# Attention ahead of two MoE layers: one transpose bank for keys and queries, kept keys, later first conversions, low parts on VectorE

## The chip, the core and the metric

The kernel runs on one core of a Trainium2 chip. The metric is the device time of one execution in microseconds. The core has TensorE (PE, matmuls; PEld are its weight loads), VectorE (DVE), ScalarE (ACT), GpSimd (POOL) and SyncE (SP, which only issues DMAs here). Each engine runs its own instructions in the order in which they stand and waits on semaphores for the others. TensorE's results go to PSUM; in this kernel VectorE and ScalarE read them from there.

## The reference

```python
# q, k, v: (2, 8, 768, 64); 4 sink keys; a window of 128
scores = scale * q @ k.T                       # causal, window 128, or one of the first 4 keys
a = softmax(where(keep, scores, -1e9)); attn = a @ v
x = attn as (1536, 512)
h = x @ w_in                                   # (512, 2048)
x = where(h >= 1, h, where(h <= -1, 0, (h + 1)**2 / 4)) @ w_out
h = x @ moe2_w_in
out = where(h > 0, h, exp(min(h, 0)) - 1) @ moe2_w_out
```

All in fp32. The four weight matrices arrive in a wider format, as pairs of 32-bit words, and are converted to fp32 on the chip.

## The kernel before

**Matmuls.** A product of the MoE is made of three passes: an operand is split into a high part (`xh`, `wh`, `gh`, a rounding to fp32r on ScalarE) and a low part (`xl`, `wl`, `gl`, the rest, a subtraction), and high x high, high x low and low x high are added up in PSUM.

**Attention (`Attn`).** Queries go in *segments* of two blocks of 128 rows: six in all, three for each of the two batches, and in each segment four *pairs* of heads. The 24 (segment, pair) *jobs* run in the order of `self.jobs`; pairs and jobs are counted from 0 here, so "pair 4" is the first pair of the second segment. A job has five stages, staggered over the jobs by a table in `stages`:

- T (`st_T`): TensorE transposes the natural blocks of keys (three blocks, the one ahead of the segment included; two in a batch's first segment) into a bank `kps` and of queries (two) into `qps`. Each bank is copied to SBUF (`kT`, `qT`; L471), by VectorE ahead of the MoE, by ScalarE later. GpSimd keeps the sink keys (`sk`, L478) and puts them behind each key block (L479).
- S0, S1 (`st_S`): scores of a query block (L504). VectorE masks them and finds the row maximum (L508), ScalarE exponentiates (L510), GpSimd copies the sinks' weights (L513).
- X (`st_X`): the weights are transposed and copied by ScalarE (L539).
- V (`st_V`): product with the values, copied to `xb` by VectorE (L565). `xb` has one buffer for all segments.

When a segment's four pairs are through, `st_sink` adds the sinks and divides (L601, L602 on VectorE), and writes the MoE's input as `xh` (L604, ScalarE) and `xl` (L605, GpSimd).

**MoE (`Moe`).** 96 items, (layer, 512 tokens, 128 of the 2048 hidden columns); item i takes 12 matmuls into `h` (L171) and 12 of item i-2 into `y` (L210), with the activation between (L178 to L188 in the first layer; L180 on VectorE ends it). The first layer needs 32 *conversion units*, each a block of a weight matrix: two ScalarE activations (L138, L139) of the loaded words `st`, and on VectorE L142, L143 and L145, which writes `F`. The items' loop asks for them three items ahead. `wsplit` makes `wh` (L158, ScalarE) and `wl` (L160: VectorE in the first 16 items, GpSimd later).

**What sets the order.** The first two segments run ahead of the MoE (`attn.spare` holds its idle PSUM banks for them). The later ones are pulled in between the MoE's matmuls, `go(n=1)` at each of some four places of an item. Ahead of the MoE TensorE's order is as written; elsewhere a list scheduler orders each engine's instructions when the program is built. The only hold on it is `issue_after`: instructions built under `self.queue(e)` are ordered behind a given one. `self.behind` holds the last exponential and the last masking of the first segment's first job; before, it is applied to unit 1 alone:

```python
after = self.behind if self.n_cv == 1 else self.own if self.n_cv > 2 * self.KF else None
```

Of the kernel before, what the change touches and what calls it, by code (L numbers as in the profile page):

```python
# [7 lines left out]
F32 = mybir.dt.float32  # L8
# [4 lines left out]
ALU = mybir.AluOpType  # L13
# [5 lines left out]
NSINK = 4  # L19
BLK = 128  # L20
KW = BLK + NSINK
# [5 lines left out]
def f32(ap):  # L27
    return ap.bitcast(F32)
# [36 lines left out]
class Moe:  # L65
# [46 lines left out]
    def queue(self, e):  # L112


        after = self.behind if self.n_cv == 1 else self.own if self.n_cv > 2 * self.KF else None
        return self.tc.issue_after(after[e]) if after else nullcontext()

    def convert(self, n):
# [163 lines left out]
class Attn:  # L282


    def __init__(self, tc, ctx, q, k, v, xts, idn, const, segs, nq=2):
        self.tc, self.nc = tc, tc.nc
        nc = self.nc
        self.q, self.k, self.v, self.xts = q, k, v, xts
        self.B, self.H, self.S, self.D = q.shape
        self.scale = 1.0 / float(self.D) ** 0.5  # L290
        self.idn, self.const = idn, const
        self.nq = nq
        pool = lambda n, b, **kw: ctx.enter_context(tc.tile_pool(name="a_" + n, bufs=b, **kw))
        self.ld_p = pool("ld", 3)
        self.qk_p = pool("qk", 2)
        self.p_p = pool("p", 4)
        self.pt_p = pool("pt", 2)
        self.xb_p = pool("xb", 1)
        self.s_p = pool("s", 2)
        self.ps = pool("ps", 2, space=PSUM)  # L300
        self.sk = {}
        self.turn, self.spare = 0, []
        self.nat = {}
        self.first = None
        self.jobs = [(s, pr) for s in segs for pr in range(self.H // 2)]
        for what in "kq":
            self.load(what, *self.jobs[0])
# [81 lines left out]
    def load(self, what, seg, pr):  # L389
        nc, D, nq = self.nc, self.D, self.nq  # L390
        b, q0 = seg[0], seg[1]
        k0 = max(q0 - 1, 0)
        nk = q0 + nq - k0
        src, r0, n = {"q": (self.q, q0, nq), "k": (self.k, k0, nk), "v": (self.v, k0, nk)}[what]
        t = self.ld_p.tile([128, n, 2, D], F32, tag=what + "n", name=what + "n")
        for j in range(2):

            (nc.scalar if what == "q" and (seg, pr) in self.jobs[:2] else nc.sync).dma_start(  # L398
                out=t[:, :, j, :],
                in_=src[b, 2 * pr + j, r0 * BLK:(r0 + n) * BLK, :].rearrange("(n p) d -> p n d", p=128))  # L400
        self.nat[what, seg, pr] = t
# [54 lines left out]
    def st_T(self, seg, pr, st):  # L456
        nc, D, nq = self.nc, self.D, self.nq
        b, q0 = seg[0], seg[1]
        qn, kn = (self.nat.pop((what, seg, pr)) for what in "qk")
        k0 = max(q0 - 1, 0)  # L460
        nk = q0 + nq - k0
        first = q0 == 0

        def parts(t, n, nm, w):

            bank = self.bank([128, n, 128], nm + "ps")
            for j in range(n):
                nc.tensor.transpose(bank[:, j, :], t[:, j].rearrange("p h d -> p (h d)"), self.idn)  # L468
            o = self.qk_p.tile([128, n, w], F32, tag=nm + "T", name=nm + "T")

            (nc.vector.tensor_copy if self.spare else nc.scalar.copy)(o[:, :, 0:BLK], bank)  # L471
            return o

        kT = parts(kn, nk, "k", KW)
        qT = parts(qn, nq, "q", BLK)
        if first:
            self.sk[pr] = self.const.tile([128, 1, NSINK], F32, tag=f"sk{pr}", name=f"sk{pr}")
            nc.gpsimd.tensor_copy(self.sk[pr], kT[:, 0:1, 0:NSINK])  # L478
        nc.gpsimd.tensor_copy(kT[:, :, BLK:], self.sk[pr].to_broadcast([128, nk, NSINK]))  # L479
        st["qk", pr] = qT, kT  # L480

    def st_S(self, seg, pr, st, n):
        nc, D, nq = self.nc, self.D, self.nq
        b, q0 = seg[0], seg[1]
        k0 = max(q0 - 1, 0)
        qT, kT = st["qk", pr]
        if n == 0:
            P = []
            nb = self.s_p.tile([128, nq, 2], F32, tag="nb", name="nb")
            st["P", pr] = P, nb  # L490
            if "sm" not in st:
                st["sm"] = self.s_p.tile([128, nq, self.H], F32, tag="sm", name="sm")
                st["ps"] = self.s_p.tile([128, nq, self.H * (NSINK + 2)], F32, tag="psn", name="psn")
        P, nb = st["P", pr]
        sm = st["sm"]
        P.append(self.p_p.tile([128, 2, WP], F32, tag="P", name="P"))
        qb = q0 + n
        ty = min(qb, 2)
        W = KW if qb == 0 else WP
        j0 = max(qb - 1, 0) - k0  # L500
        S = [self.bank([128, W], "S") for _ in range(2)]
        for h in range(2):
            hs = slice(h * D, (h + 1) * D)
            nc.tensor.matmul(S[h], lhsT=qT[hs, n, :], rhs=kT[hs].rearrange("p j k -> p (j k)")[:, j0 * KW:j0 * KW + W],  # L504
                             start=True, stop=True)
        for h in range(2):
            o = P[n][:, h, 0:W]
            dv = nc.vector.tensor_tensor_reduce(out=o, in0=S[h], in1=self.mask[ty], op0=ALU.add, op1=ALU.min,  # L508
                                                scale=-self.scale, scalar=3.0e38, accum_out=nb[:, n, h:h + 1])
            ac = nc.scalar.activation(o, o, AF.Exp, bias=nb[:, n, h:h + 1], scale=-1.0,  # L510
                                      accum_out=sm[:, n, 2 * pr + h:2 * pr + h + 1])
        sinks = st["ps"][:, n, 2 * pr * NSINK:2 * (pr + 1) * NSINK]
        nc.gpsimd.tensor_copy(sinks.rearrange("p (h s) -> p h s", h=2), P[n][:, :, BLK:KW])  # L513
        if n == nq - 1 and self.first is None:
            self.first = (ac.ins, dv.ins)

    def chunks(self, q0):
# [49 lines left out]
    def st_sink(self, seg, st):  # L567
        nc, D, nq = self.nc, self.D, self.nq
        b, q0, t, c0 = seg
        H = self.H  # L570
        R = H * NSINK
        N = nq * 128

        ps, sm = st["ps"], st["sm"]
        nc.vector.tensor_scalar(out=sm, in0=sm, scalar1=1.0e-9, scalar2=None, op0=ALU.add)
        nc.vector.reciprocal(out=sm, in_=sm)
        nc.vector.tensor_copy(ps[:, :, R:R + H].bitcast(F32R), sm)
        nc.vector.tensor_tensor(out=ps[:, :, R + H:], in0=sm, in1=ps[:, :, R:R + H], op=ALU.subtract)
        bank = self.bank([R + 2 * H, N], "sps")
        for n in range(nq):  # L580
            nc.tensor.transpose(bank[:, n * 128:(n + 1) * 128], ps[:, n, :], self.idn)
        pst = self.xb_p.tile([3 * R + 2 * H, N], F32R, tag="pst", name="pst")
        nc.scalar.copy(pst[0:R], bank[0:R])
        nc.scalar.copy(pst[2 * R:3 * R], bank[0:R])
        nc.scalar.copy(pst[3 * R:], bank[R:])
        nc.vector.tensor_tensor(out=pst[R:2 * R], in0=bank[0:R], in1=f32(pst[0:R]), op=ALU.subtract)
        xh, xl = self.xts[t]
        vs = self.vsink(b)
        yield
        for p2 in range(0, self.H // 2, 2):  # L590
            bank, rep = [self.bank([128, 2, N], nm) for nm in ("xps", "rps")]
            for j in range(2):
                h = 2 * (p2 + j)
                nc.tensor.matmul(bank[:, j, :], lhsT=vs[:, h:h + 2, :].rearrange("p h d -> p (h d)"), rhs=pst,
                                 start=True, stop=True)
            for j in range(2):
                h = 2 * (p2 + j)
                nc.tensor.matmul(rep[:, j, :], lhsT=self.one[:, h:h + 2, :].rearrange("p h d -> p (h d)"), rhs=pst,
                                 start=True, stop=True)
            x = st["xb"][:, p2:p2 + 2, :]  # L600
            nc.vector.tensor_tensor(out=x, in0=bank, in1=x, op=ALU.add)  # L601
            nc.vector.tensor_tensor(out=x, in0=x, in1=rep, op=ALU.mult)  # L602
            hi = xh[:, p2:p2 + 2, c0:c0 + N]
            nc.scalar.copy(hi, x)  # L604
            nc.gpsimd.tensor_tensor(out=xl[:, p2:p2 + 2, c0:c0 + N], in0=x, in1=f32(hi), op=ALU.subtract)  # L605
            yield


# [218 lines left out]
```

## Time and profile before

| | |
|---|---|
| time, median of 3 runs | 673.9 us (673.19 to 674.31) |
| time of the profiled execution | 674.09 us |
| its span, first to last instruction | 672.4 us |
| mean granted TensorE clock | 0.992 |
| busy: PE, PEld | 649.0 us (97%), 502.6 us (75%) |
| busy: DVE, ACT, POOL | 381.1 us (57%), 453.4 us (67%), 262.5 us (39%) |
| first 40th of the span (16.8 us): PE, ACT | 5 and 1 tenths busy |
| MoE's first matmul | at 61.19 us |

Some 61 us of attention are followed by the MoE with the rest of the attention in between. A busy share over the whole span mixes these stages; times below are from the start of the span.

### The profile page before, as it was taken

What the parts mean: (1) busy time and instruction counts of PE and PEld (TensorE: products, weight loads), DVE (VectorE), ACT (ScalarE), POOL (GpSimd) and SP (SyncE); (2) the same over time, 40 slices, a digit from 0 to 9 for tenths busy, and PEclk for the clock granted to TensorE, in tenths of its full rate; (3) what the DMA queues carried; (4) which work ended last, traced back from release to release, by engine and by line L of the source; (5) the groups of instructions that cost most, each with busy time, mean ns of one, the idle gap of its engine ahead of it and who ended that gap; (6) DMA issues with size and microseconds to landing.
All of it is one profiled execution on the core that took longest, in us unless ns stands there. A gap on an engine that the chain in (4) does not pass through costs nothing.

```text
span 672.4 us, 9284 instructions
## 1 busy us (share of the span) xinstructions
PE 649.0 (97%) x3104; PEld 502.6 (75%) x3104; DVE 381.1 (57%) x753; ACT 453.4 (67%) x928; POOL 262.5 (39%) x276
## 2 busy tenths in 40 slices
PE   5977999999999999999999999999999999999996
PEld 2665677767777767888878888888888888888884
DVE  4888999998345334223988778777432222322221
ACT  1988998997667665556868778776655555555542
POOL 2222013002114335543546555554544444444431
PEclk8899999999999999999999999999999999999999
DMA  7576564864210000000433232321010000100001
GB/s 178 133 185 177 167 180 144 223 185 122 52 24 13 13 0 1 2 0 1 156 106 115 94 97 93 100 90 61 1 62 1 0 1 0 64 1 0 1 0 68
DMA packets 71017, 48.95 MB, mean 73 GB/s; under 512 B 48944, under 2 KB 65328, under 8 KB 70960
## 3 DMA queue, kind: packets, MB, share of 16 engines
q1 hardware_dynamic: 69584, 48.00, 24.8%
q8 instruction: 26, 0.43, 0.3%
q10 hardware_dynamic: 1376, 0.26, 0.2%
q14 instruction: 31, 0.25, 0.1%
HBM read 45.11 MB, written 3.15 MB: 72 GB/s over the span
## 4 chain that ended last, share of the span: by engine, by line
PE 82%; DVE 8%; issue 3%; ACT 3%; SPq 1%; DMA 1%; POOL 1%; POOLq 0%; DVEq 0%; ACTq 0%
PE h L171 36%; PE y L210 35%; PE S L504 3%; PE ops L562 3%; PE tps L537 2%; DVE ca L143 1%; DVE P L508 1%; DVE F L145 1%; DVE wl L160 1%; DVE ca L142 1%; SPq L398 1%; PE y L267 1%; PE kps L468 1%; DVE xb L602 1%; DVE g L180 0%
## 5 line engine op out<-in xcount | busy, mean ns | idle before, releaser
L160 POOL TENSOR_TENSOR wl<-F,wh 128x512 fp32r<-128x512 f32 x160 | 219.6, 1377 | 236.7 <-ACT wh L158 220.5
L158 ACT CAST wh<-F 128x512 fp32r<-128x512 f32 x192 | 117.6, 618 | 104.4 <-PE h L171 96.2
L171 PE MATMUL h<-xh,wh 128*128 128x512 f32 x384 | 155.4, 405 | 0.3 <-DVE g L180 0.3
L171 PE MATMUL h<-xl,wh 128*128 128x512 f32 x384 | 150.7, 393 | 0.9 <-POOL xl L605 0.9
L171 PE MATMUL h<-xh,wl 128*128 128x512 f32 x384 | 151.0, 393 | 0.0
L187 ACT CAST gh<-g 128x512 fp32r<-128x512 f32 x96 | 59.6, 621 | 63.2 <-DVE g L184 36.1
L184 DVE SCALAR_TENSOR_TENSOR g<-g,h 128x512 f32<-128x512 f32 x48 | 33.0, 688 | 115.0 <-ACT g L183 115.0
L188 DVE TENSOR_TENSOR gl<-g,gh 128x512 fp32r<-128x512 f32 x96 | 68.7, 715 | 48.9 <-ACT gh L187 48.5
L171 PEld LDWEIGHTS h<-xh,wh 128*128 128x128 f32 x384 | 72.1, 188 | 20.2 <-issue 5.2
L171 PEld LDWEIGHTS h<-xh,wl 128*128 128x128 f32 x384 | 72.1, 188 | 16.7
L171 PEld LDWEIGHTS h<-xl,wh 128*128 128x128 f32 x384 | 72.2, 188 | 16.1 <-POOL xl L605 1.5
L210 PE MATMUL y<-gh,wh 128*128 128x512 f32 x192 | 79.2, 413 | 0.0
L145 DVE CUSTOM_DVE_ANT_0 F<-ca,F 128x1024 uint16<-128x1024 uint16 x64 | 73.1, 1141 | 5.2 <-DVE ca L143 1.8
L210 PE MATMUL y<-gh,wl 128*128 128x512 f32 x192 | 75.7, 394 | 0.0
L210 PE MATMUL y<-gl,wh 128*128 128x512 f32 x192 | 75.3, 392 | 0.0
L210 PE MATMUL y<-wh,gh 128*128 128x512 f32 x184 | 72.9, 396 | 0.0
L210 PE MATMUL y<-wh,gl 128*128 128x512 f32 x184 | 72.4, 394 | 0.0
L210 PE MATMUL y<-wl,gh 128*128 128x512 f32 x184 | 71.7, 389 | 0.0
L180 DVE SCALAR_TENSOR_TENSOR g<-h,g 128x512 f32<-128x512 f32 x48 | 33.0, 687 | 44.7 <-ACT g L179 44.4
L510 ACT ACTIVATE P<-P,nb 128x260 f32<-128x260 f32 (+1 forms) x96 | 46.5, 487 | 10.9 <-DVE nb L508 10.5
L513 POOL COPY psn<-P 128x8 f32<-128x8 f32 x48 | 12.1, 253 | 106.7 <-ACT P L510 101.4
L139 ACT ACTIVATE F<-st 128x512 int32<-128x512 uint32 x64 | 42.6, 669 | 12.4 <-DMA qn<-in_q_dram 11.9
(104 smaller groups left out, 911.9 us busy)
## 6 DMA issues: line engine op xcount, KB each, us to landing
st<-in_moe_w_in_dram SPq DMA_DIRECT2D x32, 512.0 KB, 3.9
st<-in_moe_w_out_dram SPq DMA_DIRECT2D x32, 512.0 KB, 3.7
kn<-in_k_dram SPq DMA_DIRECT2D x32, 96.0 KB, 2.2
vn<-in_v_dram SPq DMA_DIRECT2D x32, 96.0 KB, 2.3
out_dram<-o SPq DMA_DIRECT2D x12, 256.0 KB, 2.4
qn<-in_q_dram SPq DMA_DIRECT2D x44, 64.0 KB, 2.8
kn<-in_k_dram SPq DMA_DIRECT2D x16, 64.0 KB, 3.6
vn<-in_v_dram SPq DMA_DIRECT2D x16, 64.0 KB, 2.8
```

What stands on the lines that cost most here:

```text
L139: nc.scalar.activation(r, w0.bitcast(U32), AF.Copy, scale=2.0 ** -29)
L145: nc.vector.tensor_tensor(out=r, in0=ai, in1=r, op=ALU.add)
L158: nc.scalar.copy(hi, src)
L160: (nc.vector if i < self.KF else nc.gpsimd).tensor_tensor(out=lo, in0=src, in1=f32(hi), op=ALU.subtract)
L171: nc.tensor.matmul(h, lhsT=w[:, k * 128:(k + 1) * 128], rhs=x[:, k, c0:c0 + n], start=(k == 0 and p == 0), stop=(k == self.KD - 1 and p == 2))
L180: nc.vector.scalar_tensor_tensor(out=g, in0=h, scalar=1.0, in1=g, op0=ALU.max, op1=ALU.min)
L184: nc.vector.scalar_tensor_tensor(out=g, in0=g, scalar=-1.0, in1=h, op0=ALU.add, op1=ALU.max)
L187: ac = nc.scalar.copy(gh, g)
L188: dv = nc.vector.tensor_tensor(out=gl, in0=g, in1=f32(gh), op=ALU.subtract)
L210: nc.tensor.matmul(self.y[c], lhsT=a, rhs=b, start=(first and p == 0), stop=(last and p == 2))
L504: nc.tensor.matmul(S[h], lhsT=qT[hs, n, :], rhs=kT[hs].rearrange("p j k -> p (j k)")[:, j0 * KW:j0 * KW + W], start=True, stop=True)
L510: ac = nc.scalar.activation(o, o, AF.Exp, bias=nb[:, n, h:h + 1], scale=-1.0, accum_out=sm[:, n, 2 * pr + h:2 * pr + h + 1])
```

## The change

The blocks of keys and queries of a job are transposed into one PSUM bank and copied by one instruction into one tile `T`: entry 0 for the key block ahead, then two key blocks and two query blocks. The key block ahead is no longer loaded and transposed: it is the last key block of the same pair in the segment before, which GpSimd now copies aside (`kept`) and back into entry 0. Units 1 to 4 of the conversions are ordered behind the last exponential and the last masking of the third job (`self.jobs[2]`) instead of unit 1 behind the first. And `xl` of the segments that run ahead of the MoE is made by VectorE.

```diff
@@ Moe.queue
-        after = self.behind if self.n_cv == 1 else self.own if self.n_cv > 2 * self.KF else None
+        after = self.behind if self.n_cv <= 4 else self.own if self.n_cv > 2 * self.KF else None
@@ Attn.load
-        src, r0, n = {"q": (self.q, q0, nq), "k": (self.k, k0, nk), "v": (self.v, k0, nk)}[what]
+        src, r0, n = {"q": (self.q, q0, nq), "k": (self.k, q0, nq), "v": (self.v, k0, nk)}[what]
@@ Attn.st_T
-        def parts(t, n, nm, w):
-
-            bank = self.bank([128, n, 128], nm + "ps")
-            for j in range(n):
-                nc.tensor.transpose(bank[:, j, :], t[:, j].rearrange("p h d -> p (h d)"), self.idn)
-            o = self.qk_p.tile([128, n, w], F32, tag=nm + "T", name=nm + "T")
-
-            (nc.vector.tensor_copy if self.spare else nc.scalar.copy)(o[:, :, 0:BLK], bank)
-            return o
-
-        kT = parts(kn, nk, "k", KW)
-        qT = parts(qn, nq, "q", BLK)
+        lead = 0 if first else 1
+
+        bank = self.bank([128, 2 * nq, 128], "qkps")
+        for i, t in enumerate((kn, qn)):
+            for j in range(nq):
+                nc.tensor.transpose(bank[:, i * nq + j, :], t[:, j].rearrange("p h d -> p (h d)"), self.idn)
+        T = self.qk_p.tile([128, 1 + 2 * nq, KW], F32, tag="qkT", name="qkT")
+
+        (nc.vector.tensor_copy if self.spare else nc.scalar.copy)(T[:, 1:, 0:BLK], bank)
+        if pr not in self.kept:
+            self.kept[pr] = self.const.tile([128, BLK], F32, tag=f"kept{pr}", name=f"kept{pr}")
+        if lead:
+            nc.gpsimd.tensor_copy(T[:, 0, 0:BLK], self.kept[pr])
+        if q0 + nq < self.S // BLK:
+            nc.gpsimd.tensor_copy(self.kept[pr], T[:, nq, 0:BLK])
+        kT, qT = T[:, 1 - lead:1 + nq], T[:, 1 + nq:, 0:BLK]
@@ Attn.st_S
-        if n == nq - 1 and self.first is None:
+        if n == nq - 1 and (seg, pr) == self.jobs[2]:
             self.first = (ac.ins, dv.ins)
@@ Attn.st_sink
+        self.early = bool(self.spare)
...
-            nc.gpsimd.tensor_tensor(out=xl[:, p2:p2 + 2, c0:c0 + N], in0=x, in1=f32(hi), op=ALU.subtract)
+            (nc.vector if self.early else nc.gpsimd).tensor_tensor(out=xl[:, p2:p2 + 2, c0:c0 + N], in0=x, in1=f32(hi), op=ALU.subtract)
```

Three places where the built order differs. Line numbers of the changed program are one to three higher from `st_T` on (L510 is L511 there, L565 is L566, L604 on VectorE is the old L602).

ScalarE at the start of the program, before, from the query loads that it issues to the third pair's exponentials (`P`):

```order
L398 DMA qn<-in_q_dram 128x2x64 x4
L139 ACTIVATE F<-st 128x512
L510 ACTIVATE P,sm<-P,nb 128x132 x2
L510 ACTIVATE P,sm<-P,nb 128x260 x2
L379 CAST vpart<-vraw_190 32x64
L380 CAST vpart<-vraw_190 32x64
L138 ACTIVATE ca<-st 128x512
L510 ACTIVATE P,sm<-P,nb 128x132 x2
L510 ACTIVATE P,sm<-P,nb 128x260 x2
L539 COPY pt<-tps 128x384 x2
L139 ACTIVATE F<-st 128x512
L510 ACTIVATE P,sm<-P,nb 128x132 x2
```

and in the change, from the second pair's exponentials on:

```order
L511 ACTIVATE P,sm<-P,nb 128x132 x2
L511 ACTIVATE P,sm<-P,nb 128x260 x2
L540 COPY pt<-tps 128x384 x2
L379 CAST vpart<-vraw_192 32x64
L380 CAST vpart<-vraw_192 32x64
L511 ACTIVATE P,sm<-P,nb 128x132 x2
L511 ACTIVATE P,sm<-P,nb 128x260 x2
L540 COPY pt<-tps 128x384 x2
L138 ACTIVATE ca<-st 128x512
L139 ACTIVATE F<-st 128x512
L511 ACTIVATE P,sm<-P,nb 128x132 x2
L511 ACTIVATE P,sm<-P,nb 128x260 x2
```

These rows begin with the second pair's exponentials; ahead of them stand only the query loads, the first pair's exponentials and two small casts. Before, a conversion stood ahead of every pair's exponentials, the first pair's too; now the first two conversion activations stand behind the third pair's, ahead of pair 3's (the last two rows).

VectorE where the first segment's output is finished (L601, L602) and the next jobs go on, before:

```order
L601 TENSOR_TENSOR xb<-xps,xb 128x512 x2
L602 TENSOR_TENSOR xb<-xb,rps 128x512 x2
L471 COPY kT<-kps 128x3x128
L471 COPY qT<-qps 128x256
L508 ISA P,nb<-S,mask_152 128x260
L508 ISA nb 128x1
L508 ISA P,nb<-S,mask_152 128x260
L508 ISA nb 128x1
L565 COPY xb<-ops 128x256
```

and now:

```order
L603 TENSOR_TENSOR xb<-xps,xb 128x512 x2
L604 TENSOR_TENSOR xb<-xb,rps 128x512 x2
L469 COPY qkT<-qkps 128x4x128
L607 TENSOR_TENSOR xl_74<-xb,xh_73 128x2x256 x2
L509 ISA P,nb<-S,mask_152 128x260
L509 ISA nb 128x1
L566 COPY xb<-ops 128x256
```

Two copies have become one, and the two subtractions for `xl`, which GpSimd ran beside these rows, stand in VectorE's row ahead of the next segment's first copy into `xb`.

VectorE between the second segment's output and the MoE's first gate (L180), before:

```order
L602 TENSOR_TENSOR xb<-xb,rps 128x512 x2
L143 SCALAR_TENSOR_TENSOR ca<-st,ca 128x512
L142 TENSOR_SCALAR ca<-ca 128x512
L145 ISA F<-ca,F 128x1024
L565 COPY xb<-ops 128x256
L143 SCALAR_TENSOR_TENSOR ca<-st,ca 128x512
L142 TENSOR_SCALAR ca<-ca 128x512
L145 ISA F<-ca,F 128x1024
L143 SCALAR_TENSOR_TENSOR ca<-st,ca 128x512
L160 TENSOR_TENSOR wl_1026<-F,wh_1025 128x512
L145 ISA F<-ca,F 128x1024
L180 SCALAR_TENSOR_TENSOR g<-h,g 128x512
```

and now:

```order
L143 SCALAR_TENSOR_TENSOR ca<-st,ca 128x512
L607 TENSOR_TENSOR xl_74<-xb,xh_73 128x2x256 x2
L145 ISA F<-ca,F 128x1024
L566 COPY xb<-ops 128x256
L143 SCALAR_TENSOR_TENSOR ca<-st,ca 128x512
L160 TENSOR_TENSOR wl_1006<-F,wh_1005 128x512
L145 ISA F<-ca,F 128x1024
L160 TENSOR_TENSOR wl_1002<-F,wh_1001 128x512
L509 ISA P,nb<-S,mask_152 128x260
```

Counted from the program's start, eight conversion units were finished (L145) ahead of the first L180 before, and six now.

## Rows read from the trace of the kernel before

**Rows 1.** Busy time by stretch: us, PE (x) PEld DVE ACT POOL, clock, DMA.

```profile
70.00:162.00 92.00, 91.68 (x477) 65.59 (x476) 87.37 (x194) 85.70 (x197) 14.98 (x31) 1.00 0.62 174
...
162.00:260.00 98.00, 97.20 (x523) 70.51 (x522) 42.53 (x112) 64.03 (x149) 28.37 (x38) 1.00 0.10 23
```

**Rows 2.** Timeline at the start: start us, us, engine, line [idle before <-releaser].

```profile
9.53 0.30 DVE L508 CUSTOM_DVE_ANT_0 P<-S,mask 128x132 f32<-128x132 f32 x1
...
12.53 0.93 SPq L398 DMA_DIRECT2D qn<-in_q_dram  x2
...
15.14 0.66 ACT L139 ACTIVATE F<-st 128x512 int32<-128x512 uint32 x1 [11.89 <-DMA qn<-in_q_dram]
...
16.98 0.94 SPq L398 DMA_DIRECT2D qn<-in_q_dram  x2
...
18.24 0.63 PE L468 MATMUL kps<-idn,kn 128*128 128x128 f32 x2
...
21.79 0.69 DVE L145 CUSTOM_DVE_ANT_0 F<-ca,F 128x1024 uint16<-128x1024 uint16 x1
...
23.51 0.49 PE L468 MATMUL kps<-idn,kn 128*128 128x128 f32 x3
...
25.18 0.40 ACT L510 ACTIVATE P<-P,nb 128x132 f32<-128x132 f32 x1 [0.29 <-DVE nb L508]
```

**Rows 3.** DMA issues, 0 to 30 us: count, KB each, median us to landing.

```profile
st<-in_moe_w_in_dram SPq DMA_DIRECT2D x2, 512.0 KB, 5.7
...
qn<-in_q_dram SPq DMA_DIRECT2D x14, 64.0 KB, 2.4
```

**Rows 4.** The chain that ended last, in order of time: start us, us.

```profile
12.53 2.62 DMA qn<-in_q_dram
...
129.60 0.33 PE kps L468 x3
```

**Rows 5.** Timeline around the low parts of segments 0 and 1.

```profile
42.26 2.50 POOL L605 TENSOR_TENSOR xl<-xb,xh 128x512 fp32r<-128x512 f32 x2 [1.63 <-ACT xh L604]
...
44.80 0.42 DVE L565 COPY xb<-ops 128x256 f32<-128x256 f32 x1 [1.61 <-POOL xl L605]
...
45.83 0.42 DVE L142 TENSOR_SCALAR ca<-ca 128x512 int32<-128x512 int32 x1
...
61.13 3.04 POOL L605 TENSOR_TENSOR xl<-xb,xh 128x512 fp32r<-128x512 f32 x2 [0.88 <-ACT xh L604]
...
61.52 1.50 DVE L142 TENSOR_SCALAR ca<-ca 128x512 int32<-128x512 int32 x1
...
62.80 0.51 PE L171 MATMUL h<-xl,wh 128*128 128x512 f32 x1 [0.89 <-POOL xl L605]
...
62.95 1.78 DVE L145 CUSTOM_DVE_ANT_0 F<-ca,F 128x1024 uint16<-128x1024 uint16 x1
```

**Rows 6.** Groups by line: operation, count, busy us, mean ns, idle before.

```profile
L143 DVE SCALAR_TENSOR_TENSOR ca<-st,ca 128x512 int32<-128x512 int32 x64 | 46.1, 721 | 1.3
...
L539 ACT COPY pt<-tps 128x512 f32<-128x512 f32 (+1 forms) x48 | 24.3, 546 | 3.6 <-PE tps L537 3.4
...
L160 DVE TENSOR_TENSOR wl<-F,wh 128x512 fp32r<-128x512 f32 x32 | 23.1, 723 | 5.4 <-ACT wh L158 4.1 <-PE tps L537 1.0
...
L471 ACT COPY kT<-kps 128x384 f32<-128x384 f32 (+1 forms) x13 | 5.7, 439 | 0.4 <-PE kps L468 0.4
...
L471 DVE COPY kT<-kps 128x384 f32<-128x384 f32 (+1 forms) x11 | 5.5, 504 | 0.9 <-PE kps L468 0.8
...
L471 ACT COPY qT<-qps 128x256 f32<-128x256 f32 x13 | 4.8, 373 | 0.0
...
L471 DVE COPY qT<-qps 128x256 f32<-128x256 f32 x11 | 4.6, 416 | 0.0
...
L278 DVE COPY o<-y 128x512 f32<-128x512 f32 x6 | 4.1, 690 | 8.9 <-PE y L210 5.0 <-PE y L267 3.9
...
L718 POOL TENSOR_SCALAR_AFFINE_SELECT idn<-idn 128x128 f32<-128x128 f32 x1 | 0.3, 292 | 0.0
```

More of the change, by code (lines that the diff above doesn't have):

```diff
@@ L300, in __init__ @@
         self.ps = pool("ps", 2, space=PSUM)
-        self.sk = {}
+        self.sk, self.kept = {}, {}
         self.turn, self.spare = 0, []
@@ L459, in st_T @@
         qn, kn = (self.nat.pop((what, seg, pr)) for what in "qk")
-        k0 = max(q0 - 1, 0)
-        nk = q0 + nq - k0
         first = q0 == 0
-        def parts(t, n, nm, w):
-            bank = self.bank([128, n, 128], nm + "ps")
-            for j in range(n):
-                nc.tensor.transpose(bank[:, j, :], t[:, j].rearrange("p h d -> p (h d)"), self.idn)
-            o = self.qk_p.tile([128, n, w], F32, tag=nm + "T", name=nm + "T")
-            (nc.vector.tensor_copy if self.spare else nc.scalar.copy)(o[:, :, 0:BLK], bank)
-            return o
-        kT = parts(kn, nk, "k", KW)
-        qT = parts(qn, nq, "q", BLK)
+        lead = 0 if first else 1
[12 more added lines that the diff above has]
+        kT, qT = T[:, 1 - lead:1 + nq], T[:, 1 + nq:, 0:BLK]
         if first:
@@ L478, in st_T @@
             nc.gpsimd.tensor_copy(self.sk[pr], kT[:, 0:1, 0:NSINK])
-        nc.gpsimd.tensor_copy(kT[:, :, BLK:], self.sk[pr].to_broadcast([128, nk, NSINK]))
+        nc.gpsimd.tensor_copy(kT[:, :, BLK:], self.sk[pr].to_broadcast([128, nq + lead, NSINK]))
         st["qk", pr] = qT, kT
```

## The prediction

> **What bounds the kernel now.** I read the stretches first. From 70 to 162 us TensorE is busy for 91.68 of 92 us, VectorE for 87.37 and ScalarE for 85.70; from 162 to 260 us TensorE is still busy for 97.20 of 98, while VectorE has fallen to 42.53 and ScalarE to 64.03 [rows 1]. So from 70 us on the end is set by TensorE, and in the first of the two stretches the other two engines keep up with 4.6 and 6.3 us to spare. An edit can save time in three ways only: the MoE starts earlier, TensorE gets less to do after it, or a wait of TensorE goes.
>
> Next, the order in time at the start. VectorE's first softmax step (L508) is at 9.53, so ScalarE could run the first exponentials at about 10. It runs L139, the first weight conversion, at 15.14 after 11.89 us of idling, and only then the exponentials [rows 2]. The trace puts that wait down to a load of queries, but L139 reads `st`: the first `w_in` block, like the others in this stretch, takes some 5.7 us to land, against 2.4 for a pair's queries [rows 3]. L139 ends at 15.80, so pair 0's exponentials stand some 5.5 us behind a weight nobody needs yet. TensorE transposes pair 3 at 18.24 and pair 4 at 23.51, and pair 3's exponentials start at 25.18 [rows 2].
>
> Last, the low parts. GpSimd works on segment 0's `xl` from 42.26 for 2.50 us, and VectorE's copy into `xb` at 44.80 has waited 1.61 us for it, as `xb` has one buffer. Segment 1's run from 61.13 for 3.04 us; TensorE's first MoE matmul that reads `xl` waits 0.89 us, and under them L142 takes 1.50 us and L145 1.78 us [rows 5], where they take 0.42 [rows 5] and 0.69 [rows 2] otherwise.
>
> **The change part by part.**
>
> *Conversions behind the third pair.* The exponentials of pairs 0 and 1 move into ScalarE's idle stretch. How much comes through is set by the loads. SyncE's order does not change here. Pair 3's second query load is in by 15.15 [rows 4], so its transposes can move from 18.24 to 15.15. Pair 4's queries are issued from 16.98 [rows 2] and take 2.4 [rows 3]: 19.4 at the earliest. If TensorE needs the same 5.27 us between the two transposes as now (23.51 minus 18.24), pair 4 follows at 20.4. So pair 3's exponentials, behind pair 4 on TensorE, start 3.1 to 4.1 us earlier. Not all of it is gained. Ahead of them ScalarE's order now has two conversion activations instead of four, 2 x 0.66 = 1.3 us put off; VectorE's has none of the first unit's L142, L143 and L145, 0.42 + 0.72 + 0.69 = 1.83 us [rows 2, 5, 6]. That work comes back before or soon after the MoE begins. Net: 1.8 to 2.8 us on ScalarE, 1.3 to 2.3 on VectorE. Bounds: 0 if all comes back, 5.5 if the whole wait comes through. I take **-2.0**.
>
> *Low parts on VectorE.* Four subtractions of 0.72 us (L160 on VectorE, same shape [rows 6]) go to VectorE, +2.9 us of its time; its wait of 1.61 and the two stretchings of 1.08 and 1.09 go, -3.8 [rows 5]. At 44.8 the `xb` buffer comes free sooner: two subtractions end 1.44 us after the high parts, where GpSimd needs 2.50; of the 1.06 I take 0.6, since ScalarE also has to follow. At 62.80 TensorE's wait of 0.89 [rows 5] goes and the second low part, which ends at 64.17, comes well over 1 us sooner; I take 1.0. Together **-1.6**; bounds -0.9 (that wait alone) and -2.5 (1.61 + 0.89).
>
> *One bank for keys and queries.* Sixteen transposes go (one for each pair of the four segments that are not first in their batch); 0.33 for three is 0.11 us each [rows 4]. Twelve of them lie behind the start of the MoE, on TensorE's path: **-1.3**. The four others are hidden by ScalarE and VectorE. A copy of 128x512 out of PSUM takes VectorE 0.69 (L278) for 0.50 + 0.42 now, 11 times 0.23 = 2.5 us before the MoE; ScalarE 0.55 (L539) for 0.44 + 0.37, 13 times 0.26 = 3.4 us, two thirds of it between 70 and 162 [rows 6]. I count these at nothing on the end: they pay for work that is put off. If that cover were gone they would be worth up to 2.
>
> *The kept keys.* 32 copies of 128x128 are new on GpSimd. No row has this copy. From below, `affine_select` of the same shape takes 0.29 [rows 6]; from above, half of the two 128x512 subtractions' 2.50 is 1.25 [rows 5]. A copy has one input and the shape of the first: 0.3. In the first segment one stands between pair 0's keys and its scores, 0.3 us that vanish in the wait for pair 3's loads. In later segments the copy in waits only for its buffer, a pair ahead of its use. What can cost is VectorE being held, as it was for L142 and L145 [rows 5]. About eleven of the copies fall between 70 and 162 us. VectorE then has 24 of 32 conversion units (44 us) and some 26 L160 (19 us) to do, two thirds of its time, so up to 11 x 0.3 x 0.67 = 2.2 us. And it has two units more to catch up: eight L145 stand ahead of its first L180 now, six then, 2 x 1.83 = 3.7 us. Against 4.6 us of slack that is 1.3 too much; the 2.5 us saved on copies ahead of the MoE covers it, not fully where waits fall badly. I take **+0.5**; bounds 0 and 3.7.
>
> The Trainium skill (SBUF — State Buffer, "Who interferes with whom") says that VectorE and GpSimd share one port pair as an exclusive lock, held for a whole instruction, and that two-input VectorE operations on SBUF contend with a GpSimd operation that reads SBUF. That speaks for the low parts' move and against the kept copies; the trace agrees for L142, 1.50 for 0.42 us. By the rule alone, with each of the eleven copies holding VectorE up in full, they would cost 3.3 us (an estimate) for the 2.2 above.
>
> Sum: -2.0 - 1.6 - 1.3 + 0.5 = **-4.4 us**. The profiled execution took 674.09 us, 0.2 above the median of 673.9; 674.1 - 4.4 = **669.7 us**.
>
> **The rivals.** About 0.2% of the time, 1.35 us, is what a measurement here tells from no change.
>
> *The work comes back (20%).* VectorE's slack between 70 and 162 consists of short waits for other engines, and the 3.7 us put off do not fit into it. Then TensorE, full now, waits for gates and conversions by that much: 669.7 + 3.7 - 0.5 = 672.9, and 671.5 to 673.5 around it. For it: VectorE is at 95% there [rows 1]. Against: conversions run three items ahead of their use, and the copies get shorter on both engines.
>
> *The whole wait comes through (12%).* Loads land sooner (a key load shrinks from 96 to 64 KB) and conversions fill the gap, so that 5.5 us come instead of 2.0: 666.2. Against: pair 4's queries, whose issue doesn't move.
>
> *Slower (8%).* The kept copies hold VectorE up for longer than I think. Place: 70 to 162 us. At 1.25 us a copy, 11 x 1.25 x 0.67 = 9.2 us, 7.9 above what is free; 674.1 - 4.9 + 7.9 = 677.1. It decides from 0.8 us a copy: 5.9 us, which with the 1.3 over eats the gain and all cover. For it: 1.50 and 1.78 for L142 and L145 [rows 5]; against: the 0.29 of a like shape.
>
> **How the numbers follow.** My forecast, 668.0 to 671.5, has 60%. Faster by over 0.2% (below 672.55) are the forecast, the second rival and 0.08 of the first: 0.80. Within 0.2% lie 0.11, mostly of the first rival; slower 0.09. For eight in ten the range holds the forecast, most of the first rival and the near half of the second: **667.0 to 673.0**.
>
> **What would show it.** Right: the first exponentials near 10 us; pair 3's transposes near 15 to 16; the first MoE matmul with `xl` near 59 instead of 62.80, without a wait; L142 and L145 there at their plain 0.42 and 0.69; 96 transposes of keys and queries instead of 112; a kept copy at about 0.3 us; TensorE without new gaps from 70 to 162. Wrong: pair 3's exponentials still near 25 us (the loads or TensorE's pace bind), TensorE waiting for L180, `gl` or `wl` around 100 to 160 us, or L142 and L145 stretched all through that stretch.

## The result and the profile after

The changed kernel takes **663.0 us** (median of 4, 661.5 to 664.9) against 674.1 for the kernel before (median of 4, 673.2 to 674.3): ratio 0.9835, 95% interval 0.9807 to 0.9863. The forecast of 669.7 fell short: 11.1 us came instead of 4.4, and the time lies below the range.

The two traces are laid side by side at the same piece of work: the n-th of the 2,304 matmuls of the MoE, all 512 columns wide and in the same sequence, by their starts in both profiled executions.

| MoE matmul | before, us | after, us | earlier by |
|---|---|---|---|
| 0 (the first) | 61.19 | 58.03 | 3.2 |
| 50 | 80.52 | 75.25 | 5.3 |
| 260 | 155.57 | 151.31 | 4.3 |
| 560 | 262.53 | 256.82 | 5.7 |
| 1160 | 401.87 | 394.40 | 7.5 |
| 1760 | 540.21 | 530.40 | 9.8 |
| 2303 (the last) | 666.38 | 654.52 | 11.9 |

About half of the gain is there when attention ends, near 260 us. The other half, 6.1 us, grows steadily behind it, by 2.9 ns a matmul up to matmul 1160 and by 3.8 to 3.9 from there, where the change touches no instruction. The chain that ended last shows how: start, duration and piece, first for the kernel before, twelve matmuls a piece,

```profile
422.32 2.76 PE h L171 x12
425.08 2.77 PE y L210 x12
427.85 2.77 PE h L171 x12
430.62 2.77 PE y L210 x12
```

and then for the changed kernel:

```profile
419.95 2.72 PE h L171 x12
422.67 2.72 PE y L210 x12
425.39 2.72 PE h L171 x12
428.11 2.72 PE y L210 x12
```

From 400 to 600 us the matmuls start every 230.6 ns before and every 226.7 ns after, worked out from their starts; after, each follows in 226 or 227, before in 224 to 237. TensorE is 100% busy in both. Nearly all of this stretch is the second layer, where `y` takes `g` as the loaded weights and the weight matrix as the moving operand; in `h`, `x` moves. Its granted clock too is 1.00 (2.4 GHz) in both, so it isn't the clock. The windows of the two profiles (time, TensorE busy and instructions, granted clock, DMA share, GB/s), before first:

```profile
400.00:600.00 200.00, 200.00 (x869) 1.00 0.12 40
```

```profile
400.00:600.00 200.00, 200.00 (x885) 1.00 0.11 37
```

Sixteen more matmuls fit into the same 200 us, and no busy share tells. Ahead of that, the windows of the changed kernel that answer to [rows 1]:

```profile
70.00:162.00 92.00, 90.26 (x469) 64.11 (x467) 85.39 (x196) 83.01 (x189) 19.62 (x41) 1.00 0.58 169
162.00:260.00 98.00, 97.61 (x527) 71.36 (x527) 43.50 (x111) 63.38 (x143) 32.58 (x46) 1.00 0.09 22
```

From 70 to 162 us TensorE idles 1.7 us, where it idled 0.3 before [rows 1]. The start, from the timeline of the changed kernel, for [rows 2]:

```profile
10.42 0.40 ACT L511 ACTIVATE P<-P,nb 128x132 f32<-128x132 f32 x1 [7.17 <-DVE nb L509]
11.58 0.89 SPq L398 DMA_DIRECT2D kn<-in_k_dram  x2
16.53 0.24 ACT L379 CAST vpart<-vraw 32x64 fp32r<-32x64 f32 x1 [4.00 <-DMA vraw<-in_v_dram]
17.07 0.41 ACT L511 ACTIVATE P<-P,nb 128x132 f32<-128x132 f32 x1
17.22 0.66 PE L466 MATMUL qkps<-idn,kn 128*128 128x128 f32 x2 [2.17 <-DMA kn<-in_k_dram]
...
24.52 0.40 ACT L511 ACTIVATE P<-P,nb 128x132 f32<-128x132 f32 x1
```

and from its chain that ended last, the load of pair 3's keys (start, duration):

```profile
12.00 5.12 DMA kn<-in_k_dram
```

The first exponentials run at 10.42, but pair 1's stand at 17.07, behind a cast that waits 4.00 us for the sinks' values. Pair 3's transposes stand at 17.22, behind their keys, which are issued from 11.58 on and are in at 17.1, and pair 3's exponentials start at 24.52. Last, the start of the MoE, for [rows 5], TensorE and VectorE:

```profile
58.03 0.73 PE L171 MATMUL h<-xh,wh 128*128 128x512 f32 x2
58.60 0.48 PE L171 MATMUL h<-xl,wh 128*128 128x512 f32 x1
...
57.83 1.29 DVE L607 TENSOR_TENSOR xl<-xb,xh 128x512 fp32r<-128x512 f32 x2 [0.20 <-ACT xh L606]
59.04 0.69 DVE L145 CUSTOM_DVE_ANT_0 F<-ca,F 128x1024 uint16<-128x1024 uint16 x1
```

TensorE's wait for `xl` is gone, and L145 is at its plain 0.69.

### The profile page after: what moved, and what is told of

The parts are those of the page before. It is cut to its first block, busy times and chain, and to the rows that moved or that the text cites. A ratio compares the mean times of both kernels' runs of the same rounds, so it can differ in the third digit from the quotient of the medians.

```text
span 660.5 us, 9251 instructions
## 1 busy us (share of the span) xinstructions
PE 640.8 (97%) x3088; PEld 500.6 (76%) x3088; DVE 378.0 (57%) x746; ACT 449.9 (68%) x915; POOL 266.8 (40%) x304
## 4 chain that ended last, share of the span: by engine, by line
PE 82%; ACT 9%; DVE 3%; DMA 3%; issue 2%; POOL 0%; ACTq 0%; POOLq 0%; SPq 0%; DVEq 0%
PE h L171 37%; PE y L210 35%; PE S L505 3%; PE ops L563 2%; ACT P L511 2%; PE tps L538 2%; ACT pt L540 1%; PE qkps L466 1%; ACT ca L138 1%; ACT wh L158 1%; DMA kn<-in_k_dram 1%; ACT F L139 1%; DMA st<-in_moe_w_in_dram 1%; PE y L267 1%; DMA st<-in_moe_w_out_dram 1%
## 5 line engine op out<-in xcount | busy, mean ns | idle before, releaser
L171 PE MATMUL h<-xh,wh 128*128 128x512 f32 x384 | 153.6, 400 | 0.5 <-DVE g L180 0.5
L145 DVE CUSTOM_DVE_ANT_0 F<-ca,F 128x1024 uint16<-128x1024 uint16 x64 | 71.8, 1123 | 4.4 <-DVE ca L143 1.8
L180 DVE SCALAR_TENSOR_TENSOR g<-h,g 128x512 f32<-128x512 f32 x48 | 33.0, 687 | 44.0 <-ACT g L179 43.7
L511 ACT ACTIVATE P<-P,nb 128x260 f32<-128x260 f32 (+1 forms) x96 | 46.5, 488 | 15.0 <-DVE nb L509 12.9
L143 DVE SCALAR_TENSOR_TENSOR ca<-st,ca 128x512 int32<-128x512 int32 x64 | 47.0, 736 | 1.1
```

The costliest lines, as they stand in the source:

```text
L143: nc.vector.scalar_tensor_tensor(out=ai, in0=w1, scalar=-0x80000000, in1=ai, op0=ALU.bitwise_and, op1=ALU.bitwise_or)
L145: nc.vector.tensor_tensor(out=r, in0=ai, in1=r, op=ALU.add)
L171: nc.tensor.matmul(h, lhsT=w[:, k * 128:(k + 1) * 128], rhs=x[:, k, c0:c0 + n], start=(k == 0 and p == 0), stop=(k == self.KD - 1 and p == 2))
L180: nc.vector.scalar_tensor_tensor(out=g, in0=h, scalar=1.0, in1=g, op0=ALU.max, op1=ALU.min)
```

## The experiments

The question was where the 6.1 us behind 260 us come from. The change adds four `kept` tiles (2,048 bytes a partition), which lie ahead of `x` in SBUF, and makes the attention's pools 1,472 bytes smaller: the natural key blocks take 1,536 less, and the two buffers of `T` 64 more than those of `kT` and `qT`, since the query blocks too are 132 columns wide in `T`, not 128. So `x` moves by 2,048 bytes and the weights (`wh`, `wl`) and `gh`, `gl` by 576. Of these, 2,048 and 1,536 are multiples of 256; what is left modulo 256 is the 64 bytes of the wider `T`.

**The parts one by one, and the places alone.** *low*, *conv* and *bank* put one part of the change each into the kernel before. *pad* has none of them, only an unused tile, with every engine's instructions those of the kernel before, in the same order:

```diff
         self.p_p = pool("p", 4)
+        pad = pool("pad", 1).tile([128, 144], F32, tag="pad", name="pad")
```

Expected:

> Before with the low parts of the early segments on VectorE alone. Two things are open: what each part gives ahead of 260 us, and why the 512-column matmuls start every 226.7 ns from 260 us to the end after the change, where they started every 230.6 ns before (some 1,700 matmuls x 3.9 ns = 6.6 us). Sum theory: the low parts give 1.6 us (0.6 at 44.8, 1.0 at 62.8), so 672.5. Addresses theory (the rate hangs on where the weight and g tiles lie in SBUF; this kernel leaves them where they were): the matmuls from 260 us on stay near 230.6 ns. State theory (the rate is a state that TensorE enters or leaves by the moments at which the last attention work ends): it may fall either way, 672.5 or some 6 us less, and different executions of the kernel may differ.

> Before with the conversions of the first four units behind the third pair alone. Sum theory: 2.0 us less, 672.1; the rival in which the work comes back gives 674. Addresses theory: the tiles lie where they were, so the matmuls from 260 us on stay near 230.6 ns. State theory: either of the two rates, 672 or 666.

> Before with one bank and kept keys alone; the conversions and the low parts as before. Sum theory: 16 fewer transposes of 0.11 us, 12 of them behind the MoE's start, less 0.5 of lag: 673.3. Addresses theory: this part moves the weight and g tiles 576 bytes up, as the whole change does, so the matmuls from 260 us on start every 226.7 ns and the kernel takes about 667. State theory: either of the two.

> Before with an unused tile of 576 bytes a partition between the attention's pools, so that the weight and g tiles lie at the offsets (modulo 2,048 bytes) of the changed kernel; every engine's instructions and their order are those of before. Sum theory: 674.1, no change. Addresses theory: 226.7 ns a matmul from 260 us on, and 667 to 668. State theory: 674.1 with 230.6 ns, since no instruction's moment changes.

Measured (table below): *pad* alone takes 1.0% off, with 226.7 ns a matmul; *bank*, which moves the tiles as well, has that rate, *low* and *conv* don't. So the rate comes with the place of the tiles, not with the work. What the parts give beside it: *conv* 1.1 us; *bank*, against *pad*, 1.5 (666.4 and 667.9); *low* nothing (interval 0.9999 to 1.0018). In its profiled execution, which took 1.2 us more than its median, *low* starts the MoE 0.7 us earlier (60.45 for 61.19), and loses 3.2 us between MoE matmuls 90 and 260. Most of that stands in TensorE's waits from 95 to 160 us (total, times, longest):

```profile
PE S L504 <- ACT pt L539: 1.2, 3, 0.8
PE tps L537 <- DVE nb L508: 0.7, 1, 0.7
PE xps L595 <- DVE pst L587: 0.6, 1, 0.6
```

One profiled execution says little of such starts: *before*, *pad* and *b_pad64* (below) run the same instructions and start the MoE at 61.19, 63.36 and 60.82. The stretch from matmul 0 to 260 is steadier: 94.4, 93.5 and 94.4 us in these three, and 97.6 in *low*.

**The places undone, and the change less one part.** *a_pad64* is the changed kernel and *b_pad64* the one before, each with a pad of 64 bytes (`[128, 16]`). *a_nolow* and *a_noconv* are the changed kernel less one part:

```diff
-        after = self.behind if self.n_cv <= 4 else self.own if self.n_cv > 2 * self.KF else None
+        after = self.behind if self.n_cv == 1 else self.own if self.n_cv > 2 * self.KF else None
...
-        if n == nq - 1 and (seg, pr) == self.jobs[2]:
+        if n == nq - 1 and self.first is None:
```

> The changed kernel with an unused tile of 64 bytes a partition between the attention's pools, as in the pad run: the weight and g tiles then start at 96 modulo 128 bytes, as before the change, and not at 32. Addresses theory, with 128 bytes as what counts: the matmuls from 260 us on go back to starts every 230.6 ns, and the kernel takes about 669. If it is another part of the address than the remainder by 128, or a state that the moments of the instructions set, 663.

> Before with the unused tile of 64 bytes: the weight and g tiles at 32 modulo 128, all else as before. Addresses theory, 128 bytes: 226.7 ns a matmul from 260 us on, and 668, as with 576 bytes. If a larger part of the address counts: 674.

> The changed kernel with the low parts back on GpSimd. The tiles lie as in the changed kernel, so 226.7 ns a matmul from 260 us on. Sum theory: 1.6 us more than the changed kernel, 664.6. If the parts hinder one another as the three single ones did (low parts alone: no gain, and TensorE's waits of 1.5 us for pt, nb and pst behind 95 us): 662 to 663.

> The changed kernel with the first conversions where they were (the first unit behind the first scores, the others unbound). 226.7 ns a matmul from 260 us on. Sum theory: 2.0 us more than the changed kernel, 665; by the single run of this part (1.1 us less than before): 664.1.

Sixty-four unused bytes take 6.7 us off the kernel before and put 7.4 on the changed one. The chain of *a_pad64*:

```profile
423.39 2.80 PE h L171 x12
426.19 2.74 PE y L210 x12
428.93 2.80 PE h L171 x12
431.73 2.74 PE y L210 x12
```

Without the low parts the changed kernel is 1.2 us slower, though the two intervals overlap. Without the later conversions it is 2.3 us *faster*; the sum theory wanted 2.0 slower. The two intervals just touch (0.9810 and 0.9807), but all five executions of *a_noconv* (659.9 to 661.4) lie below all four of the changed kernel. Its MoE does start later (58.72 for 58.03; matmul 50 at 76.33 for 75.25), but it is 1.4 us ahead at matmul 260 and 1.8 to 1.9 from 380 on. TensorE's waits from 85 to 165 us, in the changed kernel and then in *a_noconv*:

```profile
PE S L505 <- ACT pt L540: 1.0, 3, 0.3
PE tps L538 <- DVE nb L509: 0.6, 1, 0.6
PE xps L596 <- DVE pst L588: 0.2, 1, 0.2
```

```profile
PE tps L538 <- DVE nb L509: 0.5, 1, 0.5
```

One of the three places with `pt`, on TensorE in the changed kernel and then in *a_noconv*:

```profile
108.51 0.70 PE L505 MATMUL S<-qkT 64*128 64x260 f32 x2
109.56 0.70 PE L505 MATMUL S<-qkT 64*128 64x260 f32 x2 [0.35 <-ACT pt L540]
110.20 0.50 PE L171 MATMUL h<-xh,wh 128*128 128x512 f32 x1
```

```profile
108.53 0.71 PE L505 MATMUL S<-qkT 64*128 64x260 f32 x4
109.17 0.50 PE L171 MATMUL h<-xh,wh 128*128 128x512 f32 x1
```

The same four score matmuls go through at once in the one; in the other the second pair is held up until ScalarE has copied `pt`, and the MoE behind it goes on 1.03 us later. It is the order and not the one execution: from matmul 0 to 260 the two profiled kernels with the changed kernel's instructions (it and *a_pad64*) take 93.3 and 94.5 us and wait three times for `pt`, and the nine with those of *a_noconv* (it and the eight below) take 90.6 to 92.9 and show no such wait.

**Which places.** These eight are *a_noconv* with pads, again with all instructions in the same order: ahead of `x` (*n_all0*, *n_both96*), between the attention's pools (*n_w64*, *n_128*), both (*n_x96*, *n_x0w32*), ahead of `gh` and `gl` alone (*n_g96*); *n_full* is *n_all0* with the attention's tiles widened so that they start at multiples of 128 bytes as well.

> The changed kernel with the first conversions where they were (the run of 660.7 us) and an unused tile of 96 bytes ahead of the x tiles: x, weights and g start at 0 modulo 128 bytes instead of 32; instructions and order are the same. If only 96 is a bad remainder: 226.7 ns a matmul from 260 us on, 660.7. If any start off 128 costs something, 32 as well: below 226.7 ns, and less than 660. If 32 alone is good: 230.6 ns and 667.

> As n_all0, and the attention's tiles that TensorE reads (transposed keys and queries, P, pt, pst) start at 0 modulo 128 too, each half of P included. Ahead of 260 us the 512-column matmuls started every 230 to 232 ns in all kernels so far, those with 226.7 ns behind it too. If that comes from the attention's tiles, some 560 matmuls up to 260 us gain 4 ns each, 2.2 us: 658.5. If it comes from the change between the two kinds of matmul, no gain over n_all0.

> The kernel of the 660.7 us run with an unused tile of 32 bytes between the attention's pools: weights and g at 64 modulo 128, x at 32 as before. If only 96 is a bad remainder (a 2,048-byte row then begins with its last 32 bytes of 128): 226.7 ns, 660.7. If the remainder by 64 counts, or 32 alone is good: 230.6 ns, 667.

> The kernel of the 660.7 us run with 64 unused bytes ahead of x and 64 between the attention's pools: x at 96 modulo 128, weights and g at 32 as in that run. If what counts is the moving operand's start: the first layer's matmuls and those of h, which read x, start every 230 ns or more, those of y, which read g and weights, every 226.7, and the kernel takes about 664. If only the weights' start counts: 660.7. If a matmul that is late makes the next ones late whatever they read: near 667.

> The kernel of the 660.7 us run with 64 unused bytes ahead of x: x, weights and g all at 96 modulo 128. Relative theory (a matmul's two operands in SBUF must start at the same remainder by 128, which remainder it is doesn't matter): 226.7 ns a matmul from 260 us on, 660.7. Absolute theory (starts at 64 and 96 are bad, 0 and 32 good): 230.6 ns or more, 667 to 669.

> The same kernel with x at 0 and the weights and g at 32 modulo 128. Relative theory: 230.6 ns or more, 667 to 669. Absolute theory: both starts are good, 226.7 ns and 660.7.

> The same kernel with 128 unused bytes between x and the weights: remainders by 128 are equal (32), those by 256 are not (160 and 32). Relative theory with 128: 226.7 ns, 660.7. Relative theory with 256 or more: 230.6 ns or more, 667 to 669.

> The same kernel with 64 unused bytes ahead of the gh and gl tiles alone: x and weights at 32, gh and gl at 96. Relative theory: h, whose operands agree, near 226.7 ns, y, whose operands don't, near 233, 667 to 669 in all. If only x against the weights counts: 226.7 ns for both, 660.7.

All runs. Starts are byte offsets in a partition, modulo 256, of `x`, of `wh`/`wl`, and of `gh`/`gl`, as the built programs list them (96 modulo 128 in the expectations is 96 or 224 here); ns is the mean distance of the matmuls' starts from 400 to 600 us in the profiled execution; times are medians.

| run | x, w, g | ns | us | ratio to before, 95% |
|---|---|---|---|---|
| before | 160, 96, 96 | 230.6 | 674.0 to 674.4 | |
| changed | 160, 160, 160 | 226.7 | 663.0 | 0.9807 to 0.9863 |
| low | 160, 96, 96 | 230.5 | 675.2 | 0.9999 to 1.0018 |
| conv | 160, 96, 96 | 230.5 | 673.3 | 0.9974 to 0.9994 |
| bank | 160, 160, 160 | 226.7 | 666.4 | 0.9865 to 0.9893 |
| pad | 160, 160, 160 | 226.7 | 667.9 | 0.9885 to 0.9913 |
| b_pad64 | 160, 160, 160 | 226.7 | 667.7 | 0.9889 to 0.9918 |
| a_pad64 | 160, 224, 224 | 230.8 | 670.4 | 0.9934 to 0.9965 |
| a_nolow | 160, 160, 160 | 226.7 | 664.2 | 0.9840 to 0.9874 |
| a_noconv | 160, 160, 160 | 226.7 | 660.7 | 0.9783 to 0.9810 |
| n_all0 | 0, 0, 0 | 226.7 | 660.2 | 0.9782 to 0.9814 |
| n_full | 0, 0, 0 | 226.7 | 658.9 | 0.9771 to 0.9797 |
| n_both96 | 224, 224, 224 | 226.7 | 661.6 | 0.9782 to 0.9831 |
| n_w64 | 160, 192, 192 | 231.1 | 668.7 | 0.9897 to 0.9933 |
| n_x96 | 224, 32, 32 | 230.8 | 669.1 | 0.9907 to 0.9935 |
| n_x0w32 | 0, 32, 32 | 231.1 | 668.1 | 0.9888 to 0.9921 |
| n_128 | 160, 32, 32 | 230.3 | 667.2 | 0.9873 to 0.9906 |
| n_g96 | 160, 160, 224 | 231.1 | 668.2 | 0.9886 to 0.9919 |

One rule fits all of these means: 226.7 ns where the three starts agree modulo 256 bytes, and 230 to 231 where they don't (by 32, 64, 128 or 192). Which remainder it is doesn't matter (0, 160 and 224 are all good). The absolute theory falls by *n_both96* and *n_x0w32*; 128 bytes as the period, which the expectations from *a_pad64* on had supposed, by *n_128*. In the changed kernel the starts of `x` and the weights differ by 256 modulo 512, so 256 is enough. That `g` against the weights counts as well as `x` against them shows in *n_g96*, where `x` and the weights agree and `g` doesn't (its line numbers are one higher):

```profile
421.83 2.75 PE h L172 x12
424.58 2.80 PE y L211 x12
427.38 2.75 PE h L172 x12
430.12 2.80 PE y L211 x12
```

Now y, which reads `g` and weights, takes 2.80 us for twelve, and h 2.75; in *a_pad64*, where `x` and weights disagree, it was h. The group whose operands agree doesn't reach 2.72 either: the disturbance runs on into its matmuls. That the slow group is the one whose operands disagree doesn't hold everywhere: in the kernel before, where only `x` disagrees with the weights, h takes 2.76 and y 2.77. So what is shown is which starts must agree, not which matmul pays. As the twelve matmuls of a group read the same two kinds of tile, the runs can't tell either whether a matmul's weights count against its own moving operand or against that of the matmul ahead. Why TensorE is slower so, and which operand waits, no run here shows.

*n_full* has the lowest time, 2.2% below before, but its interval overlaps those of *n_all0* and *a_noconv*; the attention's starts are not shown to matter. Where one MoE matmul directly follows another between 70 and 260 us, they start every 230.8 ns, as in *a_noconv* (before: 231.4), so what keeps the rate down while attention runs is something else.

## Why the prediction was wrong

**The step that failed is one that stood in the sum as nothing:** "From 70 us on the end is set by TensorE", with 1.3 us less to do, took the rest of TensorE's work to take as long as before, wherever its tiles lie. Yet the joint tile `T` is 64 bytes wider than the tiles that it replaces, which shifts the weights and `g` against `x`, and the matmuls behind 260 us start 2.9 to 3.9 ns closer together. The kept keys' tiles are not what does it, as their 2,048 bytes are a multiple of 256. In the kernel before, 64 unused bytes alone give 6.7 us (*b_pad64*). With a disagreement of 64 bytes put back (*a_pad64*) the change takes 670.4 us, 0.7 from the forecast. That it came so near is partly chance, as the terms show:

- *Conversions, -2.0.* -1.1 alone, -2.2 beside the bank (*bank* 666.4, *a_nolow* 664.2, whose intervals just overlap), and +2.3 in the whole. The first exponentials moved as forecast. Wrong was "its transposes can move from 18.24 to 15.15". Pair 3's queries were not in by 15.15 before the change either: the 2.62 us of [rows 4] are the end of L139's wait, which the prediction itself put down to `st`. The same trace has these queries landing 4.4 to 4.6 us after their issues at 12.53 and 12.98, near 17, and the keys no sooner. In the changed kernel the keys are in at 17.1, and pair 3's exponentials start 0.7 us earlier (24.52 for 25.18), not 3.1 to 4.1. Of the 5.3 us that are gained at matmul 50, 1.0 is lost again by matmul 260, in waits for `pt`, `nb` and `pst`, although some of the saved transposes lie in that stretch: the sign "TensorE without new gaps" failed.
- *Low parts, -1.6.* The waits went as said. The worth depends on the other parts: nothing alone, 1.2 us in the whole, and 5.7 beside the bank without the later conversions (*bank* 666.4, *a_noconv* 660.7). The three parts, each alone and *bank* against *pad*, add up to -1.7 us, and the whole without the rate (*a_pad64*) gives -4.1: they can't be added.
- *One bank and kept keys, -1.3 and +0.5.* -1.5 measured against *pad*, for -0.8. There are 96 transposes, and a kept copy takes 0.44 us aside and 0.36 back, for the 0.3 assumed and the 0.8 from which the slower rival was to decide, so that rival is out. The transposes, from the view of the tile `qkps` (count, then least, median and longest ns, first and last start):

```profile
L466 PE MATMUL qkps<-idn,kn x48: 270/272/477, 5.4 to 224.6; 128*128 128x128 f32 x48
L466 PE MATMUL qkps<-idn,qn x48: 272/273/447, 6.6 to 224.8; 128*128 128x128 f32 x48
```

and the copies, from the groups by line (busy us, mean ns, idle before):

```profile
L475 POOL COPY kept<-qkT 128x128 f32<-128x128 f32 x16 | 7.0, 435 | 26.3 <-ACT qkT L469 15.6 <-DVE qkT L469 10.6
L473 POOL COPY qkT<-kept 128x128 f32<-128x128 f32 x16 | 5.7, 357 | 18.0 <-PE S L505 17.8
```

- *The rivals.* "The whole wait comes through" gave 666.2, nearest in number, but by loads that didn't come sooner. "The work comes back" is half right: work came back as waits of TensorE, not at the gates and conversions that it named.

*conv* against the kernel before, and *a_noconv* against the changed kernel, differ in nothing but the order in which the same instructions stand, so their -1.1 and -2.3 us are the order's. Not settled: which of the moved instructions holds TensorE's `pt`, `nb` and `pst` back, by 1 to 3 us between 90 and 165 us. The waits are seen, but no run moved one instruction alone.

## What to carry to other kernels

Where TensorE bounds the end, lay both traces side by side at the same matmul: a gain that grows steadily behind the last edited instruction is a rate, and a busy share of 100% hides it. An edit that adds, drops or resizes a tile can move the tiles behind it, as here, so run the old kernel with the new places (one unused tile) before crediting the edit; here that control alone gave 6.5 of 11.1 us. And try the same start modulo 256 bytes for both SBUF operands of a matmul stream: the kernel before gains 1.0% by one line.

## What the runs showed of the hardware

A stream of weight loads and 512-column fp32r matmuls at a granted clock of 1.00 starts every 226.7 ns where the SBUF starts of the moving operand and of the loaded weights agree modulo 256 bytes, and every 230 to 231 ns on average where one kind of pair disagrees: 2.80 us for the twelve that disagree and 2.74 or 2.75 for the next twelve in *a_pad64* and *n_g96*, 2.76 and 2.77 in the kernel before. No other size or type was tried. The Trainium skill (SBUF — State Buffer, "Who interferes with whom") gives TensorE two independent read ports, one for the moving operand and one for the weights; a reader would take from that that the place of one against the other costs nothing, and these runs differ from it. Its figure for isolated matmuls of 512 columns, about 216 ns (TensorE: Matmul & The Clock Gate, "Back-to-back issue gap"), lies 11 ns below the best that this kernel shows; the figure that the same section has for a sustained stream of weight loads and such matmuls, about 131 ns, lies further off, and no run here comes near it.
